# The opening constants of an mLSTM and mixture-of-experts kernel: moved between engines, built in another way, and all step ranks chosen anew

## The chip, the core and the metric

The kernel runs on one core of a Trainium2 chip. The metric is the device time of one execution in microseconds (us). The engines are named as the profile names them: PE is TensorE, DVE is VectorE (V in the code), ACT is ScalarE (A), POOL is GpSimd (G), and SP is SyncE, which here only issues DMAs.

## What is computed

Three layers in a row on 4 x 768 tokens: an mLSTM attention with 8 heads of 40, a leaky two-layer network with 2048 hidden units, and a top-1 mixture of 8 experts with 1024 hidden units. Cut to what matters here:

```python
for t in range(S):                      # _attn_ref, B=4, H=8, S=768, D=40
    m_new = np.maximum(f_gate[:, :, t] + m, i_gate[:, :, t])
    f_stab = np.exp(f_gate[:, :, t] + m - m_new)
    i_stab = np.exp(i_gate[:, :, t] - m_new)
    m = m_new
    C = f_stab * C + i_stab * outer(vt, kt)
    n = f_stab * n + i_stab * kt
    y[:, :, t] = sigmoid(o_gate[:, :, t]) * (C @ qt) / max(abs(n . qt), 1)

h = x @ w_in                            # _moe_ref, x: 3072 x 320, d_ff 2048
x2 = (max(h, 0) + alpha * min(h, 0)) @ w_out

xn, en = normalised x2, normalised expert_emb     # _moe2_ref, 8 experts
e = argmax(xn @ en.T / tau)
out = softmax weight of e * (max(x2 @ w1[e], 0) @ w2[e])
```

The recurrence over t is not run step by step: the gates of all 32 (batch, head) rows go through two scans, and the attention then works on chunks of 128 tokens, with a decay matrix that is the exponential of an argument made on PE.

## The kernel before

The 3072 tokens are 24 chunks of 128 (`NCH`), six for each of the four batches. Each chunk passes through the attention steps (`plan_chunk`: `load`, `loadt`, `mrow`, `arg0`, `arg1`, `exp0`, `exp1`, `s`, `p0`, `p1`, `phi`, `plo`, `u`, `c`, `o`, `tot`, `y`, `xhi`, `xlo`, `xt`). The transposed result goes to the first dense network (`m1` against `w_in_p`, `m2` against `w_out_p`, chunks taken in groups of one or two), then to the router, and after a sort by expert to the slots of the second network (`e1`, `e2`). Matrix factors are split into a high and a low half-precision part, so that DVE, ACT and POOL have work for every PE step. The weights of the first network arrive as 8-byte floats and are turned into 4-byte ones on DVE: `pconv` (its instructions stand in `to_f32`, on lines 632, 634 and 636) takes two pieces, that is six DVE instructions; there are 5 such pairs of `w_in` (512 columns a piece) and 8 pairs of `w_out` (320 columns a piece). The experts' weights are prepared later in 56 units (`ul`, `uh`, `uo`, `us`).

**The opening.** Before any planned step, the function issues instructions that write constants, in the order of the source. An engine takes its instructions in the order issued.

- POOL: `ident` and `iot` (lines 238 to 243), then `argL` filled with 0 and its first 27 rows with 1 (lines 371, 372), the two `argR` tiles, each a fill and three selections of 128 x 1024 (lines 374 to 377), `eye` and `low` (lines 378 to 384), one `qk` tile, `cf`, `vs`, `xs`, `x2s`, `ones`, `tri` and more, and last, because `g_set()` is called at line 1288 just before the plan is made, the gates' constants `keep` and `r0` (lines 277 to 279).
- DVE: four small instructions that need `iot`, then two `qk` tiles (line 388).
- SP and ACT begin with DMAs.

`argL` and `argR` are the two factors of the decay argument: `argL` gets three row groups from DRAM in `g_rows` and `argR` gets three rows in `mrow`, the rest of them is constant.

**The gates.** `g_load` brings `f_gate` and `i_gate`. `g_scan` on DVE (lines 291 to 295) multiplies by `keep` and adds `r0` in its scans. From it follow `g_top`, `g_res`, `g_mid`, `g_low` (three bf16 parts of two vectors), `g_store` to DRAM (line 311), `g_rows` back into `argL` (line 315), and beside it `g_w`, `g_wexp`, `g_wt`, `g_wt2`, `g_dec`, `g_dec2`. No `arg` step can run before `g_rows`, and the first `m1` needs the first chunk's `xt`.

**The order.** All steps after the opening are put in order by `Plan.order()` while the program is being written; at run time each engine simply takes its steps in that order and waits where data is late. The planner keeps a time for each engine, begins these clocks at `START`, and at each turn takes, among the steps that could start within `AHEAD` = 0.03 us of the first one, the one with the largest rank. A step's rank is its longest remaining path by the plan's own costs, plus `lean(k)`: `LEAN[name]`, plus `SOON[name]` if the step's index is below 4, plus `FIRST[name]` if it is below 2. `PACE` adds to the rank along the chain of the experts' units, `UNITS` gives the earliest planned time of each unit's load, and `EARLY` is a gap on a link from each `xt` to the first `m1` of its group:

```python
first_of = {k: rank[k] + lean(k) for k in steps}
...
plan.link(("xt", i), ("m1", chunk_group[i][0], 0), EARLY if i > 3 else 0.0)
```

Of the kernel before, what the change touches and what calls it, by code (L numbers as in the profile page):

```python
# [9 lines left out]
F32 = mybir.dt.float32  # L10
# [3 lines left out]
ALU = mybir.AluOpType  # L14
# [4 lines left out]
P = 128  # L19
B, H, S, D = 4, 8, 768, 40  # L20
# [20 lines left out]
class Plan:  # L41
# [7 lines left out]
    START = {"T": 0.5, "V": 2.0, "A": 2.0, "G": 4.9, "S": 1.2}  # L49
# [104 lines left out]
    "alpha": -35.4, "alpha2": -17.1, "arg0": 37.2, "arg1": 40, "c": -45.5, "cd": 75.6, "consts": 48.9, "e1":  # L154
    -115.6, "e2": -110.4, "ehi": 141.4, "elo": -9.4, "eout": -111.3, "ep": 81.6, "exp0": 58.9, "exp1": 15.6,
    "ey": 136.4, "g_dec": 51.6, "g_dec2": 33, "g_load": 150, "g_low": 2.9, "g_mid": -81.7, "g_res": -148.1,
    "g_rows": 115.9, "g_scan": 18.2, "g_store": -150, "g_top": 149.8, "g_w": 56.8, "g_wexp": -47.5, "g_wt":
    74.6, "g_wt2": 93.9, "gate": 147.1, "lane": -48.9, "lanes": -124.3, "load": 54.7, "loadt": 97.7, "logits":
# [3 lines left out]
    "psplit": -62.9, "rank": 38.5, "rexp": 71.5, "rload": -12.6, "rnorm": -63.7, "rsq": 150, "s": 84.9,  # L162
# [19 lines left out]
}  # L182
FIRST = {
    "alpha": -15.8, "alpha2": -80, "arg0": 54.7, "arg1": -22.7, "c": -80, "cd": 19.3, "consts": 69.7, "e1": 2,
    "e2": 80, "ehi": -29.6, "elo": 6.4, "eout": 68.2, "ep": -33.9, "exp0": 39.2, "exp1": 59.4, "ey": -9.1,
    "g_dec": -8.5, "g_dec2": 7.7, "g_load": -80, "g_low": -72.3, "g_mid": -56.1, "g_res": -4.9, "g_rows":
    -68.4, "g_scan": 7.4, "g_store": -23.2, "g_top": 80, "g_w": 80, "g_wexp": 24, "g_wt": -51.8, "g_wt2": -80,
    "gate": -77.9, "lane": 21.6, "lanes": 0.2, "load": 70.7, "loadt": -45.9, "logits": -57.1, "m1": 76.5,
    "m1f": 25.5, "m1h": 29.5, "m1l": 0.7, "m1r": -80, "m2": 80, "max": 69.2, "mrow": 80, "norm": -80, "norm2":
    22.6, "o": -35.1, "open": 25.2, "p0": -66.5, "p1": 80, "pconv": 49.1, "phi0": 69.8, "phi1": 43.2, "plo0":  # L190
    73, "plo1": -75.6, "pload": 80, "plow": 57.8, "pput": 45.1, "psplit": 13.3, "rank": 18, "rexp": -30.8,
    "rload": 75.9, "rnorm": -11.9, "rsq": 79.6, "s": -28.8, "scale": -59.9, "sort0": 22.8, "sort1": -80,
# [16 lines left out]
def kernel(  # L209
# [24 lines left out]
    ctx.enter_context(tc.manual_schedule())  # L234

# [4 lines left out]
                    pattern=[[-1, 32]], channel_multiplier=1)  # L240
# [23 lines left out]
    gt = {}  # L264

    def g_set():
# [83 lines left out]
    gp_ = ctx.enter_context(tc.tile_pool(name="gp", bufs=2))  # L350
# [7 lines left out]
    qk = [att.tile([P, 2, H // 2, P], F32, name=f"qk{i}") for i in range(NQ)]  # L358
# [20 lines left out]
    G.affine_select(out=eye, in_=eye, compare_op=ALU.not_equal, fill=1.0, base=0,
                    pattern=[[-1, P]], channel_multiplier=1)  # L380
# [460 lines left out]
    def x2_zero():  # L841
# [9 lines left out]
                    pattern=[[1, P]], channel_multiplier=-1)  # L851
# [132 lines left out]
    lane = const.tile([P, NCH], F32, name="lane")  # L984
# [303 lines left out]
    g_set()  # L1288
# [141 lines left out]
```

## Time and profile before

| | us |
|---|---|
| median of 3 runs | 736.11 |
| the runs | 735.71, 736.11, 743.06 |
| the profiled execution | 738.54 |
| its span, first to last instruction | 736.8 |
| PE busy | 639.4 (87%) |
| DVE busy | 464.5 (63%) |
| POOL busy | 362.2 (49%) |
| ACT busy | 335.4 (46%) |

The span lies inside the profiled execution's own time; 1.7 us lie around it. Times in the rows further down count from the start of the span. A busy share of the whole span says little here, since the kernel has stages: the opening and the gates, a stretch in which weights are converted and the first chunks go through, a long stretch of dense work on PE, and a tail of scattered writes.

### The profile page before, as it was taken

The page shows a single profiled execution, that of the slowest core. Times are in us where ns is not written, and L with a number is a line of the kernel's source. Part 1 is how long each engine was busy: PE and PEld are TensorE (multiplying, and loading weights), DVE is VectorE, ACT ScalarE, POOL GpSimd, SP SyncE. Part 2 cuts the span into 40 slices and gives each one's busy share as a digit, 9 for nine tenths or more (in the row PEclk, how much of TensorE's full clock was granted, in tenths as well). Part 3 has the DMA queues.
Part 4 walks back from the last instruction along what each step waited for, and adds up shares of the span by engine and source line. Part 5 has one row for each costly group of instructions (what it writes and reads, how often), then busy time and mean ns, then how long its engine had stood idle before and what let it go on. Part 6 is the DMA issues. An engine that isn't in the chain of part 4 may idle for free. (4 is left out here: it accounts for less than half of the span.)

```text
span 736.8 us, 17794 instructions
## 1 busy us (share of the span) xinstructions
PE 639.4 (87%) x6903; PEld 525.7 (71%) x6903; DVE 464.5 (63%) x1113; ACT 335.4 (46%) x666; POOL 362.2 (49%) x433
## 2 busy tenths in 40 slices
PE   0037567899999999989999999999999999999995
PEld 0024465677878778768878888887788887888884
DVE  1896988586889978966879887895346121121211
ACT  1335565455755675655575666533222222222221
POOL 9774769564655655635454645535311332323321
PEclk9999789899999999999999999999999999999999
DMA  8255534258669978788877875548755999999843
GB/s 269 91 166 125 168 115 137 81 165 216 222 198 215 247 228 210 211 188 240 225 228 195 254 196 168 140 149 267 213 183 161 266 252 302 360 326 315 214 120 64
DMA packets 109225, 149.02 MB, mean 202 GB/s; under 512 B 72215, under 2 KB 84416, under 8 KB 105298
## 3 DMA queue, kind: packets, MB, share of 16 engines
q1 hardware_dynamic: 81730, 83.22, 43.2%
q10 hardware_dynamic: 24128, 54.54, 23.6%
q0 software_dynamic: 3280, 10.10, 4.4%
q8 instruction: 56, 0.92, 0.5%
q14 instruction: 31, 0.25, 0.1%
HBM read 143.57 MB, written 30.46 MB: 236 GB/s over the span
## 5 line engine op out<-in xcount | busy, mean ns | idle before, releaser
L742 PE MATMUL hp<-xt,w_in_p 128*128 128x256 f16 (+1 forms) x1664 | 186.4, 267 | 19.9 <-DVE r L755 16.0
L742 PEld LDWEIGHTS <-w_in_p 128*128 128x128 f16 x1664 | 151.7, 99 | 43.2 <-DVE r L755 17.7
L762 POOL TENSOR_TENSOR g<-r,g 128x512 f16<-128x512 f32 (+1 forms) x104 | 118.2, 1141 | 118.8 <-ACT g L759 111.9
L830 PE MATMUL o<-w_out_p,g 128*128 128x320 f16 x1152 | 170.8, 302 | 2.7 <-DVE r L755 2.2
L830 PEld LDWEIGHTS <-g 128*128 128x128 f16 x1152 | 112.4, 99 | 48.6 <-DVE r L755 2.9
L755 DVE SCALAR_TENSOR_TENSOR r<-r,al,hp 128x256 f32<-128x256 f32 (+1 forms) x208 | 85.3, 453 | 30.5 <-ACT r L749 30.3
L1216 DVE SCALAR_TENSOR_TENSOR h<-hp,h 128x512 f16<-128x512 f32 x48 | 32.7, 689 | 112.6 <-ACT h L1212 103.3
L759 ACT ACTIVATE g<-r 128x512 f16<-128x512 f32 (+1 forms) x104 | 61.7, 594 | 70.3 <-DVE r L755 59.3
L749 ACT ACTIVATE r<-hp 128x512 f32<-128x512 f32 (+1 forms) x104 | 57.9, 557 | 46.0 <-PE hp L742 41.1
L1227 PEld LDWEIGHTS <-h 128*128 128x128 f16 x648 | 61.5, 98 | 23.3 <-ACT h L1212 1.1
L480 POOL TENSOR_TENSOR ph<-mb,ph 128x512 f16<-128x512 f32 x48 | 65.4, 1369 | 25.1 <-ACT ph L477 21.1
L1233 POOL DMA_INDIRECT out_dram<-y,idx x27 | 27.5, 1017 | 82.1 <-DMA out_dram<-y,idx 64.1
L1212 ACT ACTIVATE h<-hp 128x512 f16<-128x512 f32 x48 | 28.1, 596 | 81.6 <-PE hp L1207 76.8
L1182 POOL DMA_INDIRECT xg<-x_d,idx x31 | 30.5, 984 | 60.1 <-ACT y L1230 51.6
L1207 PEld LDWEIGHTS <-wr 128*128 128x128 f16 x896 | 51.5, 98 | 1.8 <-issue 0.5
L1207 PEld LDWEIGHTS <-w_in_p 128*128 128x128 f16 x832 | 48.0, 98 | 3.5 <-issue 2.2
L1207 PE MATMUL hp<-xt,w_in_p 128*128 128x128 f16 x768 | 46.1, 219 | 1.9 <-DMA xt<-xg 1.4
L1207 PE MATMUL hp<-xt,wr 128*128 128x128 f16 x768 | 46.1, 219 | 0.2 <-DMA xt<-xg 0.2
L1227 PE MATMUL o<-w_out_p,h 128*128 128x320 f16 x288 | 42.2, 299 | 0.2 <-issue 0.2
L1227 PE MATMUL o<-wr,h 128*128 128x320 f16 x288 | 42.1, 299 | 0.0
L552 POOL TENSOR_TENSOR y<-y,rd 128x320 f32<-128x320 f32 x24 | 19.6, 816 | 34.9 <-DVE y L547 29.3
L477 ACT ACTIVATE ph<-mb 128x512 f16<-128x512 f32 x48 | 29.6, 625 | 10.7 <-DVE mb L472 7.1
(206 smaller groups left out, 1036.3 us busy)
## 6 DMA issues: line engine op xcount, KB each, us to landing
wr<-wp SPq DMA_DIRECT2D x32, 1280.0 KB
w_in_p<-wp SPq DMA_DIRECT2D x15, 1280.0 KB
w_out_p<-wp SPq DMA_DIRECT2D x15, 1280.0 KB
kvo_t<-in_kvo_dram SPq DMA_DIRECT2D x24, 576.0 KB
ust<-in_moe_w_dram ACTq DMA_DIRECT2D x32, 320.0 KB
wp<-wo ACTq DMA_DIRECT2D x32, 320.0 KB
ust<-in_moe_w_dram ACTq DMA_DIRECT2D x16, 512.0 KB
wp<-wo ACTq DMA_DIRECT2D x16, 512.0 KB
```

Of the source, the lines that this page charges most:

```text
L477: A.activation(st["P", i][:, 0, j], st["mb", i][:, j], AF.Copy)
L480: G.tensor_tensor(st["P", i][:, 1, j], st["mb", i][:, j], st["P", i][:, 0, j], ALU.subtract)
L742: T.matmul(hp[:, a, :n], lhsT=w_in_p[:, wk, f], rhs=xt[:, xk], start=z == 0, stop=z == 7)
L749: A.activation(r, e_t[j, m], AF.Relu, scale=-1.0)
L755: V.scalar_tensor_tensor(r[:, a], r[:, a], al1[:, m + a:m + a + 1], hp[:, a], ALU.mult, ALU.add)
L759: A.activation(g_t[j][:, 0, m:m + 2], e_t[j, m], AF.Copy)
L762: G.tensor_tensor(g_t[j][:, 1, m:m + 2], e_t.pop((j, m)), g_t[j][:, 0, m:m + 2], ALU.subtract)
L830: T.matmul(o[:, :DM], lhsT=g[:, gi, k, tt], rhs=w_out_p[:, k, a], start=z == 0, stop=z == 47)
L1182: G.indirect_dma_start(out=xg, out_offset=None, in_=src, in_offset=bass.IndirectOffsetOnAxis(ap=idx[:, j:j + 1].bitcast(U32), axis=0))
L1207: T.matmul(hp[:, m], lhsT=w[:, wk, f], rhs=xt[:, xk], start=z == 0, stop=z == 7)
L1216: V.scalar_tensor_tensor(hs[:, 1], hp, 0.0, hs[:, 0], ALU.max, ALU.subtract)
L1227: T.matmul(o, lhsT=h[:, hi, k], rhs=w[:, k, a], start=z == 0, stop=z == 23)
```

## The change

- `START`, the planner's beginning times, go from V 2.0, A 2.0, G 4.9, S 1.2 to V 7.0, A 1.0, G 8.0, S 1.0.
- All of `LEAN`, `SOON` and `FIRST`, and `PACE` (5.15 to 6.16), `UNITS` ((121.6, 5.63) to (115.5, 5.75)) and `EARLY` (-1055.3 to -1184.1) have new values.
- `g_set()` is called right behind its definition, ahead of the other constants, and its three fills are on DVE. The pool `gp_` is opened earlier for it.
- `argL` is filled on DVE. `argR` is no longer filled and selected on POOL at full size: POOL fills a 128 x 8 tile `ind` and makes three selections on it, and DVE copies it, broadcast over 128 columns, into both `argR` tiles.
- The `qk` tiles 0 and 1 are filled on DVE, tile 2 on POOL, behind `ind` (before: 1 and 2 on DVE, 0 on POOL).

```diff
-    START = {"T": 0.5, "V": 2.0, "A": 2.0, "G": 4.9, "S": 1.2}
+    START = {"T": 0.5, "V": 7.0, "A": 1.0, "G": 8.0, "S": 1.0}
...
 LEAN = {
-    60, "m1": 18.6, "m1f": 149, "m1h": -51.5, "m1l": -14.3, "m1r": 105.8, "m2": 18.6, "max": -7.4, "mrow":
-    145.1, "norm": -66.9, "norm2": -112.7, "o": 54.3, "open": -150, "p0": 53.4, "p1": -44.8, "pconv": -48.3,
...
+    "max": 135.6, "mrow": 33.5, "norm": -34.1, "norm2": 127.7, "o": 11.5, "open": 21.6, "p0": -138.9, "p1":
+    25.6, "pconv": -49.4, "phi0": 118.8, "phi1": 112.6, "plo0": 74.1, "plo1": 122.4, "pload": -19.6, "plow":
...
 SOON = {
-    "norm": -16.7, "norm2": -70.9, "o": -80, "open": -65.6, "p0": 80, "p1": 70.8, "pconv": 73.3, "phi0": -80,
...
+    -62.3, "o": 23.2, "open": -3.2, "p0": 35, "p1": 61.3, "pconv": 22.9, "phi0": 28.8, "phi1": -14, "plo0":
...
 FIRST = {
-    22.6, "o": -35.1, "open": 25.2, "p0": -66.5, "p1": 80, "pconv": 49.1, "phi0": 69.8, "phi1": 43.2, "plo0":
...
+    "norm": 77.1, "norm2": -57.9, "o": 4.6, "open": -80, "p0": -80, "p1": 76.1, "pconv": 65.1, "phi0": 62.8,
...
-PACE = 5.15
-UNITS = (121.6, 5.63)
+PACE = 6.16
+UNITS = (115.5, 5.75)
...
-EARLY = -1055.3
+EARLY = -1184.1
...
+    gp_ = ctx.enter_context(tc.tile_pool(name="gp", bufs=2))
...
-        G.memset(gt["keep"], 1.0)
-        G.memset(gt["keep"].rearrange("p (c t) -> p c t", t=P)[:, :, 0:1], 0.0)
-        G.memset(gt["r0"], 0.0)
+        V.memset(gt["keep"], 1.0)
+        V.memset(gt["keep"].rearrange("p (c t) -> p c t", t=P)[:, :, 0:1], 0.0)
+        V.memset(gt["r0"], 0.0)
+
+    g_set()
...
-    gp_ = ctx.enter_context(tc.tile_pool(name="gp", bufs=2))
...
-    G.memset(argL, 0.0)
-    G.memset(argL[0:27], 1.0)
-    for x in argR:
-        G.memset(x, 0.0)
-        for k in range(3):
-            G.affine_select(out=x, in_=x, compare_op=ALU.not_equal, fill=1.0, base=-8 * k,
-                            pattern=[[-1, H], [0, P]], channel_multiplier=1)
+    for x in qk[:2]:
+        V.memset(x, 0.0)
     G.memset(eye, 0.0)
...
-    for x in qk[:1]:
+    ind = const.tile([P, H, 1], F32, name="ind")
+    G.memset(ind, 0.0)
+    for k in range(3):
+        G.affine_select(out=ind, in_=ind, compare_op=ALU.not_equal, fill=1.0, base=-8 * k,
+                        pattern=[[-1, H], [0, 1]], channel_multiplier=1)
+    V.memset(argL, 0.0)
+    V.memset(argL[0:27], 1.0)
+    for x in argR:
+        V.tensor_copy(x, ind.to_broadcast([P, H, P]))
+    for x in qk[2:]:
         G.memset(x, 0.0)
-    for x in qk[1:]:
-        V.memset(x, 0.0)
...
-    g_set()
     add(("g_load",), "S", 0.85, g_load, dma=0.6)
```

## Rows read from the trace of the kernel before

**Rows 1.** The page: the span, and PE in 40 slices, in tenths.

```profile
span 736.8 us, 17794 instructions
PE   0037567899999999989999999999999999999995
```

**Rows 2.** Busy time by stretch: start:end, length, PE, PEld, DVE, ACT, POOL, PEclk, DMA.

```profile
0.00:21.00 21.00, 0.00 (x0) 0.00 (x0) 2.35 (x7) 2.12 (x3) 19.55 (x43) 1.00 0.85 262
21.00:81.00 60.00, 22.94 (x154) 15.90 (x155) 51.05 (x81) 25.89 (x49) 37.66 (x34) 0.95 0.48 131
81.00:140.00 59.00, 42.54 (x496) 34.98 (x496) 48.19 (x116) 33.16 (x84) 44.07 (x100) 0.85 0.39 117
140.00:680.00 540.00, 525.37 (x5657) 434.04 (x5655) 353.30 (x898) 261.84 (x509) 244.84 (x244) 1.00 0.79 224
680.00:737.00 57.00, 48.57 (x604) 40.73 (x600) 9.59 (x14) 12.35 (x22) 16.11 (x17) 0.97 0.54 140
```

**Rows 3.** Timeline, POOL in the opening: start, us, instruction, idle before.

```profile
1.28 2.65 POOL L371 MEMSET argL<- 128x3072 bf16 x1
...
7.60 3.42 POOL L376 TENSOR_SCALAR_AFFINE_SELECT argR<-argR 128x1024 bf16<-128x1024 bf16 x3
...
15.34 0.20 POOL L378 MEMSET eye<- 128x128 bf16 x1
...
20.02 0.14 POOL L853 IOTA rev<- 128x8 f32 x1
...
20.15 0.73 POOL L277 MEMSET gates_a<- 32x768 f32 x1
20.94 0.10 POOL L278 MEMSET gates_a<- 32x6 f32 x1
20.98 0.73 POOL L279 MEMSET gates_a<- 32x768 f32 x1
```

**Rows 4.** Timeline, DVE in the same stretch.

```profile
2.11 0.91 DVE L388 MEMSET qk<- 128x1024 f32 x1 [0.16 <-issue]
3.19 0.91 DVE L388 MEMSET qk<- 128x1024 f32 x1 [0.16 <-issue]
4.04 0.06 DVE L291 MEMSET gates_a<- 32x1 f32 x1
21.07 1.75 DVE L292 TENSOR_TENSOR_SCAN gates_a<-gates_a 32x768 f32<-32x768 f32 x1 [16.97 <-POOL gates_a L278]
```

**Rows 5.** Timeline, single DVE instructions after the opening.

```profile
47.10 0.33 DVE L875 MEMSET ep<- 128x320 uint32 x1
...
48.12 0.21 DVE L882 CAST ep<-em 8x128 f16<-8x128 f32 x1
...
52.29 0.41 DVE L632 TENSOR_SCALAR w<-wst 128x512 int32<-128x512 int32 x1
...
64.81 0.50 DVE L536 COPY tot<-op 128x328 f32<-128x328 f32 x1 [1.17 <-PE op L518]
```

**Rows 6.** DMA queues from 0 to 12 us: packets, MB, share.

```profile
q10 hardware_dynamic: 476, 1.69, 48.2%
q1 hardware_dynamic: 322, 1.16, 36.2%
```

**Rows 7.** Timeline: storing the gates, the first argument, the first m1.

```profile
40.15 3.09 SPq L311 DMA_DIRECT2D pc_d<-gates_a  x1
...
56.11 0.58 PE L439 MATMUL ap<-argR,argL 128*128 128x512 bf16 x1 [6.99 <-DMA argL<-pc_d]
...
80.93 1.86 PE L742 MATMUL hp<-xt,w_in_p 128*128 128x128 f16 x16 [3.62 <-ACT mb L448]
```

**Rows 8.** DVE groups by line and shape, 20 to 145 us: busy, mean ns.

```profile
L634 DVE SCALAR_TENSOR_TENSOR w<-wst,w 128x320 int32<-128x320 int32 x16 | 9.8, 654 | 0.0
...
L632 DVE TENSOR_SCALAR w<-wst 128x320 int32<-128x320 int32 x16 | 8.5, 573 | 0.0
...
L636 DVE SCALAR_TENSOR_TENSOR w<-wst,w 128x320 int32<-128x320 int32 x16 | 8.2, 553 | 0.0
```

More of the change, by code (lines that the diff above doesn't have):

```diff
@@ L153 @@
 LEAN = {
[L154 to L158, printed above, removed]
[3 rows of a table removed]
@@ L162 @@
-    "psplit": -62.9, "rank": 38.5, "rexp": 71.5, "rload": -12.6, "rnorm": -63.7, "rsq": 150, "s": 84.9,
[4 rows of a table removed]
+    "alpha": 150, "alpha2": 111.9, "arg0": -42.1, "arg1": -22.1, "c": 12.3, "cd": -127.5, "consts": -37.5,
+    "e1": -117.8, "e2": -27.1, "ehi": 117.1, "elo": -12.1, "eout": -93.7, "ep": 93, "exp0": 51.5, "exp1":
+    -85.8, "ey": 64.4, "g_dec": -70.5, "g_dec2": 140.3, "g_load": -8.4, "g_low": -25.6, "g_mid": -22.1,
+    "g_res": 136, "g_rows": 3.5, "g_scan": -136, "g_store": -150, "g_top": -126.8, "g_w": -33.5, "g_wexp":
@@ L167 @@
+    -148.7, "g_wt": 127, "g_wt2": -143.3, "gate": 52.5, "lane": 112.3, "lanes": -71.9, "load": -23.1, "loadt":
[3 rows of a table added]
+    -126.5, "pput": -7.5, "psplit": 100.9, "rank": -29.4, "rexp": 10.4, "rload": -150, "rnorm": 116.3, "rsq":
[4 rows of a table added]
 }
 SOON = {
-    "alpha": 32.9, "alpha2": 51.1, "arg0": -17.9, "arg1": -62.5, "c": -49.1, "cd": 80, "consts": -15.3, "e1":
-    -12.9, "e2": -15, "ehi": -80, "elo": -8.8, "eout": 80, "ep": -11.7, "exp0": 49.6, "exp1": 5.4, "ey":
-    -64.5, "g_dec": -26.1, "g_dec2": -46, "g_load": -20.6, "g_low": -54.3, "g_mid": 80, "g_res": -61.2,
@@ L172 @@
-    "g_rows": -36.9, "g_scan": 70, "g_store": 34.8, "g_top": -80, "g_w": -43.9, "g_wexp": -58.7, "g_wt":
-    -20.6, "g_wt2": 71.4, "gate": -4.8, "lane": -78, "lanes": 41.1, "load": -46.3, "loadt": -77.6, "logits":
-    2, "m1": 32.5, "m1f": 70.1, "m1h": -57.9, "m1l": 29.9, "m1r": -76.6, "m2": 78.2, "max": 80, "mrow": 5,
-    "norm": -16.7, "norm2": -70.9, "o": -80, "open": -65.6, "p0": 80, "p1": 70.8, "pconv": 73.3, "phi0": -80,
-    "phi1": 80, "plo0": 39.1, "plo1": 9.6, "pload": 34.8, "plow": 58.7, "pput": -64, "psplit": -68.5, "rank":
@@ L177 @@
-    -7.9, "rexp": -79.6, "rload": 79.8, "rnorm": -34.3, "rsq": 29.7, "s": 48.9, "scale": -6.5, "sort0": 80,
[4 rows of a table removed]
+    "alpha": 0.3, "alpha2": 55.5, "arg0": 80, "arg1": -13.2, "c": -76.1, "cd": 80, "consts": 69.8, "e1": -75,
+    "e2": 80, "ehi": -1.9, "elo": 55.2, "eout": -31.5, "ep": -31.6, "exp0": -41.5, "exp1": -38.4, "ey": 54.9,
+    "g_dec": 2.9, "g_dec2": 80, "g_load": 43, "g_low": 74.5, "g_mid": -73.7, "g_res": -57.2, "g_rows": 80,
+    "g_scan": -28.5, "g_store": 49.2, "g_top": -51.9, "g_w": 74.8, "g_wexp": 50, "g_wt": 6.5, "g_wt2": 68.8,
@@ new lines @@
+    "gate": -20.4, "lane": 77.8, "lanes": -28.8, "load": -80, "loadt": -4.4, "logits": 14.2, "m1": 80, "m1f":
+    -80, "m1h": 62, "m1l": -61.5, "m1r": -20.8, "m2": 5.6, "max": 76.8, "mrow": -80, "norm": -24.3, "norm2":
+    -62.3, "o": 23.2, "open": -3.2, "p0": 35, "p1": 61.3, "pconv": 22.9, "phi0": 28.8, "phi1": -14, "plo0":
+    64.2, "plo1": 80, "pload": 53.6, "plow": 8.3, "pput": -80, "psplit": -53.3, "rank": -20.2, "rexp": 30.8,
+    "rload": 53.2, "rnorm": -61.7, "rsq": -38.9, "s": 68.1, "scale": 27, "sort0": -71.6, "sort1": -6.3,
[4 rows of a table added]
@@ L182 @@
 }
 FIRST = {
[L184 to L188, printed above, removed]
@@ L189 @@
-    "m1f": 25.5, "m1h": 29.5, "m1l": 0.7, "m1r": -80, "m2": 80, "max": 69.2, "mrow": 80, "norm": -80, "norm2":
-    22.6, "o": -35.1, "open": 25.2, "p0": -66.5, "p1": 80, "pconv": 49.1, "phi0": 69.8, "phi1": 43.2, "plo0":
-    73, "plo1": -75.6, "pload": 80, "plow": 57.8, "pput": 45.1, "psplit": 13.3, "rank": 18, "rexp": -30.8,
-    "rload": 75.9, "rnorm": -11.9, "rsq": 79.6, "s": -28.8, "scale": -59.9, "sort0": 22.8, "sort1": -80,
[3 rows of a table removed]
+    "alpha": -26.9, "alpha2": -28.1, "arg0": 50.2, "arg1": 37.2, "c": -80, "cd": -60.3, "consts": 80, "e1":
@@ new lines @@
+    -56.3, "e2": 69, "ehi": -52.9, "elo": 80, "eout": 36.9, "ep": 25.3, "exp0": -48.3, "exp1": 63.7, "ey":
+    68.1, "g_dec": -56.9, "g_dec2": -45.2, "g_load": -42, "g_low": -49, "g_mid": 49.2, "g_res": 43.1,
+    "g_rows": -11, "g_scan": -0.9, "g_store": 53.3, "g_top": 80, "g_w": 55.3, "g_wexp": -57, "g_wt": -62.6,
+    "g_wt2": -5.6, "gate": -72.4, "lane": 80, "lanes": 58.1, "load": -70.2, "loadt": -9.3, "logits": -80,
+    "m1": 80, "m1f": 80, "m1h": 46.5, "m1l": -13.9, "m1r": 19.8, "m2": -19.2, "max": 38.2, "mrow": -41.2,
@@ L196 @@
+    "norm": 77.1, "norm2": -57.9, "o": 4.6, "open": -80, "p0": -80, "p1": 76.1, "pconv": 65.1, "phi0": 62.8,
+    "phi1": 18, "plo0": -80, "plo1": 16.7, "pload": 47.7, "plow": -35.5, "pput": 23.5, "psplit": -53.2,
+    "rank": 18.6, "rexp": -34.3, "rload": 73.9, "rnorm": 80, "rsq": 0.4, "s": -80, "scale": 41.4, "sort0": 80,
[4 rows of a table added]
 }
 LOOK = 3.6
-PACE = 5.15
-UNITS = (121.6, 5.63)
+PACE = 6.16
+UNITS = (115.5, 5.75)
 SORTS = ((12, 4), 0)
 WARM = (12, 3)
-EARLY = -1055.3
+EARLY = -1184.1
 CHUNK = ("load", "loadt", "mrow", "arg0", "arg1", "exp0", "exp1", "vhi", "vlo",
```

25 rows, old and new, of tables (FIRST, LEAN, SOON) are left out of this document.

## The prediction

> **What bounds the kernel now.** I read the slices of the page first [rows 1]: PE has two empty slices, then four half-filled ones, and is at 9 tenths from the ninth slice on to the last. The busy time by stretch says it in numbers [rows 2]. From 140 to 680 us PE is busy 525.4 of 540 us at a granted clock of 1.00, which is its upper level, 2.4 GHz: there PE is the bound, and only 14.6 us are idle. From 680 on 8.4 us are idle. Before 140 us PE is idle 140 - 22.9 - 42.5 = 74.5 us. So three quarters of all PE idle time (97.5 us) lies in the front, and there another engine sets the pace.
>
> In the first 21 us that engine is POOL: busy 19.6 us, while DVE has 2.4 us of work and PE none [rows 2]. The timelines show why. POOL works through its constants from the top; the argL and argR tiles alone fill it from 1.28 to 15.34 us, and the gates' constants come last, from 20.15 to 21.7 us [rows 3]. DVE has filled its qk tiles by 4.1 us and then stands 16.97 us in front of the gate scan, released by POOL's line 278 [rows 4]. (The page's releaser is exact enough: the other operand, r0 on line 279, is first read by the later scan.) Nothing else on DVE can pass the scan, because an engine keeps its order, so the conversions of weights wait behind it too.
>
> From 21 to 140 us DVE is busy 51.1 + 48.2 = 99.2 of 119 us [rows 2], the busiest of the five there. The scan at 21.07 leads to the store of the gates at 40.15, to the first argument at 56.11 and the first m1 at 80.93 [rows 4, 7]. A stretch with one engine 83% busy and a chain of dependent steps in it can be shifted as a whole; that is the base of the forecast.
>
> **The change part by part.** *DVE's new opening.* Up to 2.11 us nothing changes (four small instructions that need iot). Then, in the order of the new source:
>
> - keep, 768 elements; its 6 columns; r0, 768. The two fills on DVE that the trace has are 1024 elements in 0.91 us and 320 in 0.33 us [rows 4, 5]: 0.83 ns an element and 0.06 us fixed. So 0.70 + 0.06 + 0.70, with the fixed part for the 6 columns: 1.5 us. POOL's 0.73 for the same shape [rows 3] agrees.
> - two qk tiles, as before: (4.04 - 2.11) / 2 = 0.97 us each [rows 4], 1.9 us.
> - argL with zeros. 3072 two-byte elements. The ep fill is 640 two-byte zeros in the code and stands in its row as 320 elements of uint32 [rows 5], so 1536 elements: 1.34 us. If it is not so rewritten, 2.62 us.
> - argL's 27 rows with 1.0: between 1.34 us, if this too is done in pairs, and 2.62 us for 3072 elements one by one. I take 2.62, because the only rewritten fill in a row is one of zeros; on POOL, argL, which is filled twice, takes 2.65 us [rows 3].
> - two argR copies, 1024 elements, f32 to bf16. The trace has no such copy. Lower bound: the CAST of 128 elements in 0.21 us and the one-source instruction of 512 in 0.41 us [rows 5] give 0.52 ns an element, so 0.68 us. Upper bound: the copy of 328 elements from PSUM in 0.50 us [rows 5], 1.5 ns an element, so 1.6 us. Source and target lie in SBUF as in the first two, so I take 0.68, both 1.4 us.
>
> Sum: 2.11 + 1.5 + 1.9 + 1.34 + 2.62 + 1.4 = 10.9 us, and with the one-column fill of line 291 the scan starts at 10.95 instead of 21.07. **The scan is 10.1 us earlier.** Cheapest values everywhere: 9.6 us on the clock, 11.5 earlier. Dearest (zeros 2.62, copies 1.6 each): 14.0 us, 7.1 earlier.
>
> The ones deserve a second look: by the Trainium skill, page VectorE: DVE Perf Modes, section Zero memsets can be issued as uint32 (trn2), a fill takes a cycle per element whatever the type, and only a fill of zero can be issued as uint32. The ep row agrees for zero, and no row here shows the case of ones. By the rule the scan starts at 10.95, and if it did not hold, at 9.7; the forecast would be 1.3 us lower.
>
> *POOL.* Taken off: everything from 1.28 to 15.34 us, 14.1 us, and the gates' 1.55 us [rows 3]. Added: ind, a fill and three selections of 128 x 8, at 0.14 us by the IOTA of that size [rows 3], about 0.6 us. POOL's remaining opening, from 15.34 to 20.15, takes 4.8 us. POOL is then through at 1.28 + 4.8 + 0.6 = 6.7 us. Its work hides behind DVE's 10.9 us; if it were not hidden it would only matter for ind, which DVE reads at 9.5 us and which is written ahead of the qk and cf fills, near 3 us. So the copies wait for nothing.
>
> *What is late next at the scan.* The gate loads: f_gate, issued at 0.81, had landed by 4.04, since the fill of line 291 overwrites its first column [rows 4]. In the new order SP may issue the loads of qk, which wait for DVE's fills up to 5.5 us, ahead of the gates; even then two issues and at most the 3.2 us to landing seen before end ahead of 10.9. Behind the scan, the first conversion needs two pieces of 512 KB: by 12 us each of the two hardware queues had moved more than that (1.69 and 1.16 MB) [rows 6]. Neither takes the scan's place as the bound.
>
> *What the argL and argR work costs on DVE.* 5.4 us of the 10.9 stand ahead of the scan for tiles whose rows arrive only before 56.11 [rows 7]. This is the part of the opening that is not gained.
>
> *The planner's numbers.* START issues nothing; it only moves the plan's clocks. EARLY changes nothing at all: each xt already precedes that m1 by a dependency, whose term in the rank is larger than one with a gap below -1000, before and after. LEAN, SOON, FIRST, PACE and UNITS add and remove no instruction; they reorder every queue (SP's and ACT's with their DMAs too). PE's work is the same, so a new order is worth what it does to the 97.5 us of PE idle time. The long stretch has at most 14.6 us to give. I put the new order at nothing, with both signs open, and keep the width for the range.
>
> *The sum.* The shift of 10.1 us passes through to the end, because the front is a DVE-bound chain and the stretch behind it is PE-bound without another clock of its own. The profiled execution, 738.54, would come to 728.4. It lies 2.4 us above the median of the runs; from the median: 736.11 - 10.1 = **726.0 us**.
>
> **The rivals.**
>
> *The order gives more.* The front still holds 64 us of PE idle time after the shift. An order that feeds PE there 8% better wins 5 us more: 721 us. For it: in the front DVE keeps 20 of 119 us free [rows 2]. Against: DVE's work there has to be done in any order.
>
> *The order gives the gain back.* Its place is DVE's queue between the gates and the first xt. The lean of p0 of chunk 0 is 53.4 + 80 - 66.5 = 66.9 before and -138.9 + 35 - 80 = -183.9 after; that of the w_out conversions stays near -49. So where both can start, conversions now go ahead of the first chunk's product, which no m1 can do without. The eight pairs take 9.8 + 8.5 + 8.2 = 26.5 us, 3.3 a pair [rows 8]. Three pairs more ahead of p0 make 9.9 us: 736 us, no change. For it: the size of that swing, 251 us. Against: a conversion done early needn't be done later, and DVE is 82% busy from 81 to 140 us [rows 2], so most of it comes back.
>
> *Slower.* The same mechanism, with the time not given back. The first m1 then comes later than now. Two pairs stay below 1%; slower by 7.4 us takes 10.1 + 7.4 = 17.5 us, so from 5.3 pairs on. With six pairs: 736.1 - 10.1 + 19.9 = 745.9 us.
>
> *The scan doesn't move.* That needs a wait on something other than POOL up to 21 us; the loads above leave no room for it. I give it nothing of its own.
>
> **How the numbers follow.** About 1% (7.4 us) is what a measurement of this kernel can tell from no change; that is 728.7 and 743.5 us. The shift with a neutral order, 721 to 731 us: 0.47, of which 0.09 lie above 728.7 (the dear end of DVE's opening alone gives 729). The better order, below 721: 0.19. The gain given back, 731 to 743.5: 0.22. Slower: 0.12. So faster 0.38 + 0.19 = 0.57, the same 0.09 + 0.22 = 0.31, slower 0.12. The likeliest case has 721 to 731 as its own range. The range for 8 in 10 runs from 715 to 742 us: it leaves out the far end of the better order and nearly all of the slower case.
>
> **What would show it.** In the profile after: the scan of line 292's counterpart at 10 to 14 us, with DVE busy and not waiting ahead of it; the ones fill at 2.6 us, and the argR copies at 0.7 (over 1.1 would be the upper row's kind); POOL's opening ended near 7 us; the store of the gates near 30, the first argument near 46 and the first m1 near 71 us; PE idle before 140 us at about 64. Wrong would be: a scan near 11 us and a first m1 that is not earlier (then the new queue order took it, to be seen in what DVE does between them), or a front that is 10 us shorter and a stretch behind it with well over 14.6 us of PE idle time.

## The result and the profile after

The changed kernel took 727.97 us (median of 6 runs, 727.02 to 729.69), against 736.76 us for the kernel before on the same chip (median of 6, 731.94 to 743.06). The ratio is 0.9883, with a 95% interval from 0.9834 to 0.9932, that is 5.0 to 12.2 us. Ratios are estimated without the few runs that fell in a slower state, so they differ a little from the quotient of two medians (0.9881 here). So it is faster, by 8.8 us between the medians; 726.0 had been forecast, and the range 715 to 742 holds it.

The page after: the span, and PE in 40 slices (compare [rows 1]).

```profile
span 728.0 us, 17810 instructions
PE   0137568999999989999999999999989999999995
```

Busy time by stretch after (start:end, length, then PE, PEld, DVE, ACT, POOL, each with its number of instructions, PEclk, DMA share, GB/s), for [rows 2]:

```profile
0.00:21.00 21.00, 2.77 (x16) 2.27 (x16) 16.00 (x24) 2.97 (x3) 8.23 (x36) 1.00 0.79 210
21.00:81.00 60.00, 26.62 (x196) 19.76 (x197) 50.33 (x89) 28.86 (x57) 39.18 (x38) 0.86 0.63 178
81.00:140.00 59.00, 45.04 (x517) 38.54 (x517) 48.40 (x111) 35.28 (x87) 39.23 (x100) 0.82 0.51 131
140.00:680.00 540.00, 529.31 (x5689) 436.35 (x5687) 356.36 (x888) 259.09 (x503) 248.36 (x239) 0.99 0.79 220
680.00:728.00 48.00, 39.26 (x494) 33.35 (x491) 7.60 (x11) 10.23 (x18) 12.53 (x13) 0.95 0.58 155
```

Before 140 us PE is now idle 140 - 2.77 - 26.62 - 45.04 = 65.6 us instead of 74.5: 8.9 less. In the long stretch it is idle 10.7 us instead of 14.6, and behind it 8.7 instead of some 8.2. Against these 12.4 us of idle time that are gone stand 3.6 us more of busy time (643.0 against 639.4): the granted clock of the two stretches from 21 to 140 us is 0.86 and 0.82, where it was 0.95 and 0.85 [rows 2], so the same work takes longer there. That makes the 8.8 us between the two spans. It is one execution of each; two later profiled executions of the same kernel, on other chips, had spans of 736.5 and 735.3 us, so the split is good to some us only, and what follows goes by medians.

DVE's opening after: start, us, instruction, idle before and its releaser (compare [rows 4]).

```profile
2.05 0.70 DVE L279 MEMSET gates_a<- 32x768 f32 x1
...
4.91 0.91 DVE L375 MEMSET qk<- 128x1024 f32 x1 [0.16 <-issue]
6.09 1.34 DVE L388 MEMSET argL<- 128x1536 uint32 x1 [0.27 <-issue]
8.12 2.62 DVE L389 MEMSET argL<- 27x3072 bf16 x1 [0.69 <-DVE argL L388]
10.67 1.21 DVE L391 CAST argR<-ind 128x1024 bf16<-128x1024 f32 x2
13.59 0.17 DVE L1291 TENSOR_SCALAR al<-al 128x16 f32<-128x16 f32 x1 [1.71 <-DMA al<-in_moe_alpha_dram]
13.98 0.06 DVE L295 MEMSET gates_a<- 32x1 f32 x1 [0.21 <-DMA gates_a<-in_f_gate_dram]
14.07 1.75 DVE L296 TENSOR_TENSOR_SCAN gates_a<-gates_a 32x768 f32<-32x768 f32 x1
```

DVE works from 2 us on without a long pause, and POOL's opening constants end at 7.1 us (6.7 had been forecast). But the scan starts at 14.07, 7.0 us earlier than before [rows 4], not 10.1. Two waits stand ahead of it that the kernel before didn't have: for alpha, the leak of the first network, and for `f_gate`. SP's queue after shows why:

```profile
0.81 0.47 SPq L1288 DMA_DIRECT2D al<-in_moe_alpha_dram  x1
1.34 3.53 SPq L286 DMA_DIRECT2D gates_a<-in_f_gate_dram  x1
...
38.11 0.45 SPq L315 DMA_DIRECT2D pc_d<-gates_a  x1
```

The new ranks put the load of alpha first on SP, and its DVE instruction ahead of the scan. The load is issued at 0.81 and its reader goes at 13.59; the next issue on the queue, `f_gate`'s, takes 3.53 us, and its data too is there only near 13.98. (That alpha is the cause is shown further down, by moving it.) Before, alpha was loaded at 36.78 us.

From the scan to the first m1, after (DVE, POOL, PE, SP and ACT; [rows 7] has the counterparts of before):

```profile
19.01 3.84 POOL L325 TENSOR_TENSOR gates_b<-gates_b 32x640 f32<-32x640 f32 x1
...
21.65 4.33 DVE L305 SCALAR_TENSOR_TENSOR gates_a<-gates_b,gates_a 32x768 f32<-32x768 f32 x1
25.91 1.90 DVE L305 SCALAR_TENSOR_TENSOR gates_b<-gates_b,gates_a 32x768 f32<-32x768 f32 x1
...
47.56 0.63 PE L444 MATMUL ap<-argR,argL 128*128 128x512 bf16 x1
...
49.28 0.69 DVE L477 SCALAR_TENSOR_TENSOR mb<-sp,mb 128x512 f32<-128x512 f32 x1 [4.95 <-ACT mb L453]
...
66.84 1.22 SPq L571 DMA_TRANSPOSE xt<-xs  x1
...
81.00 0.47 ACT L647 ACTIVATE w<-w 128x320 f32<-128x320 f32 x1 [3.94 <-DVE w L641]
...
82.46 0.57 ACT L453 ACTIVATE mb<-ap 128x512 f32<-128x512 f32 x1
...
83.08 1.87 PE L747 MATMUL hp<-xt,w_in_p 128*128 128x128 f16 x16 [3.49 <-ACT mb L453]
```

The store comes at 38.11 (2.0 us earlier than before), the first argument at 47.56 (8.6 earlier), the first transposed chunk at 66.84 (8.4 earlier, it was 75.23), and the first m1 at 83.08, 2.2 us *later* than before. So the first m1 does not simply follow its own chunk. In the new order PE makes the attention of three chunks ahead of it, where it made two; by 81 us it has been busy 29.4 us with 212 matmuls instead of 22.9 us with 154 [rows 2]. And the row of m1 says what PE waits for at the end: `mb` on ACT (L453), which reads `ap`; the code gives `ap` and the product of m1 the same five buffers. On ACT that `mb` stands behind a pair of `w_out` conversions, for which ACT itself waits 3.94 us. Before, the first m1 waited for `mb` in the same way [rows 7], behind a pair of `w_out` too:

```profile
78.85 0.47 ACT L642 ACTIVATE w<-w 128x320 f32<-128x320 f32 x1 [3.48 <-DVE w L636]
```

But that was the first such pair, and now it is the third.

Two questions follow. Does the end follow the scan, as the forecast says, although m1 does not? And what do the new ranks do, which the forecast put at nothing?

### The profile page after: what moved, and what is told of

Its sections match the earlier page's. It is cut to its first block, busy times and chain, and to the rows that moved or that the text cites. A ratio compares the mean times of both kernels' runs of the same rounds, so it can differ in the third digit from the quotient of the medians.

```text
span 728.0 us, 17810 instructions
## 1 busy us (share of the span) xinstructions
PE 643.0 (88%) x6903; PEld 530.3 (73%) x6903; DVE 478.7 (66%) x1120; ACT 336.4 (46%) x666; POOL 347.5 (48%) x424
## 5 line engine op out<-in xcount | busy, mean ns | idle before, releaser
L747 PE MATMUL hp<-xt,w_in_p 128*128 128x256 f16 (+1 forms) x1664 | 190.0, 271 | 16.3 <-DVE r L760 7.3
L747 PEld LDWEIGHTS <-w_in_p 128*128 128x128 f16 x1664 | 153.7, 101 | 40.2 <-DVE r L760 14.5
L767 POOL TENSOR_TENSOR g<-r,g 128x512 f16<-128x512 f32 (+1 forms) x104 | 122.6, 1185 | 112.2 <-ACT g L764 109.2
L485 POOL TENSOR_TENSOR ph<-mb,ph 128x512 f16<-128x512 f32 x48 | 62.9, 1318 | 36.7 <-ACT ph L482 33.4
L1212 PEld LDWEIGHTS <-w_in_p 128*128 128x128 f16 x832 | 48.3, 98 | 1.4
L462 PE MATMUL sp<-qk 64*128 64x128 f32 x384 | 30.9, 301 | 18.9 <-DMA qk<-in_qk_t_dram 16.5
L462 PEld LDWEIGHTS sp<-qk 64*128 64x128 f32 x384 | 25.9, 201 | 26.0 <-DVE gates_a L296 16.5
```

The source lines that it names most:

```text
L462: T.matmul(sp[:, r, z], lhsT=x[w, 1, z], rhs=x[w, 0, z], start=True, stop=True)
L485: G.tensor_tensor(st["P", i][:, 1, j], st["mb", i][:, j], st["P", i][:, 0, j], ALU.subtract)
L747: T.matmul(hp[:, a, :n], lhsT=w_in_p[:, wk, f], rhs=xt[:, xk], start=z == 0, stop=z == 7)
L767: G.tensor_tensor(g_t[j][:, 1, m:m + 2], e_t.pop((j, m)), g_t[j][:, 0, m:m + 2], ALU.subtract)
L1212: T.matmul(hp[:, m], lhsT=w[:, wk, f], rhs=xt[:, xk], start=z == 0, stop=z == 7)
```

## The experiments

Every kernel was timed beside the kernel before on its own chip, and the ratios are to that. Times in the middle columns are starts from the profiled execution, in us.

| kernel | first scan | store issued | first argument | first m1 | median | ratio (95%) |
|---|---|---|---|---|---|---|
| before | 21.07 | 40.15 | 56.11 | 80.93 | 736.76 | 1 |
| after | 14.07 | 38.11 | 47.56 | 83.08 | 727.97 | 0.9883 (0.9834 to 0.9932) |
| open_only | 11.94 | 31.13 | 46.95 | 71.77 | 724.66 | 0.9851 (0.9798 to 0.9904) |
| ranks_only | 21.07 | 45.17 | 54.62 | 90.32 | 737.15 | 1.0028 (0.9990 to 1.0067) |
| alpha_late | 11.95 | 35.98 | 45.44 | 81.26 | 726.28 | 0.9895 (0.9839 to 0.9951) |
| delay_scan | 25.82 | 50.10 | 59.30 | 94.83 | 742.22 | 1.0092 (1.0053 to 1.0130) |
| light_opening | 5.88 | 33.49 | 45.55 | 70.38 | 731.07 | 0.9900 (0.9849 to 0.9950) |
| alpha_far | 11.94 | 31.02 | 47.49 | 72.31 | 730.32 | 0.9880 (0.9822 to 0.9937) |
| light_and_far | 5.88 | 27.79 | 44.81 | 69.62 | 727.86 | 0.9836 (0.9787 to 0.9884) |
| after_again | 14.15 | 39.99 | 49.45 | 85.27 | 733.56 | 0.9912 (0.9873 to 0.9950) |
| open_only_2 | 11.94 | 31.03 | 47.76 | 72.58 | 725.52 | 0.9856 (0.9804 to 0.9909) |
| after_3 | 13.80 | 37.88 | 47.29 | 82.59 | 729.43 | 0.9899 (0.9849 to 0.9949) |
| gates_only | 5.88 | 34.86 | 49.91 | 74.74 | 726.09 | 0.9843 (0.9791 to 0.9894) |
| act_copies | 5.88 | 26.22 | 42.10 | 66.92 | 718.10 | 0.9752 (0.9703 to 0.9800) |

The kernel before took 736.76 us (median) beside after, 734.57 beside open_only to delay_scan, 740.30 beside light_opening to after_again, and 736.92 beside the last four. Medians from different groups of these are therefore not compared. One kernel's times in the middle columns differ too from one execution to the next: the first m1 of the changed kernel by up to 2.7 us (three profiles), that of open_only by 0.8 (two).

### The change cut in two: the opening alone, the ranks alone

open_only is the changed kernel with the planner's old numbers, ranks_only the kernel before with the new ones:

```diff
-    START = {"T": 0.5, "V": 7.0, "A": 1.0, "G": 8.0, "S": 1.0}
+    START = {"T": 0.5, "V": 2.0, "A": 2.0, "G": 4.9, "S": 1.2}
...
-PACE = 6.16
-UNITS = (115.5, 5.75)
+PACE = 5.15
+UNITS = (121.6, 5.63)
```

> The new opening with all planner numbers of before, so the planned steps stand in the order of before. The alpha load is then late in SP's queue, and the scan should start when DVE's opening ends, near 11.9 us instead of 21.07. Theory shift (the whole program follows the scan): 736.8 - 9.1 = 727.6 us. Rival order (the gain of the change is the new order's, the front swallows an earlier scan): within 1% of the kernel before, 733 to 740 us.

> The old opening with all planner numbers of after, so the planned steps stand in the order of after. POOL's constants release the scan at about 21.1 us. Theory shift: the change moved the scan from 21.07 to 14.07, 7.0 us, of the 8.8 us that it gained, so the order alone is worth 1.8 us: about 735 us. Rival order: 728 us, as after.

open_only, timelines of DVE, POOL, SP and PE:

```profile
11.94 1.75 DVE L295 TENSOR_TENSOR_SCAN gates_a<-gates_a 32x768 f32<-32x768 f32 x1
...
16.89 6.38 POOL L324 TENSOR_TENSOR gates_b<-gates_b 32x640 f32<-32x640 f32 x1
...
20.33 0.94 DVE L304 SCALAR_TENSOR_TENSOR gates_a<-gates_b,gates_a 32x768 f32<-32x768 f32 x1
...
31.13 2.75 SPq L314 DMA_DIRECT2D pc_d<-gates_a  x1
...
46.95 0.58 PE L443 MATMUL ap<-argR,argL 128*128 128x512 bf16 x1 [6.94 <-DMA argL<-pc_d]
...
71.77 1.86 PE L746 MATMUL hp<-xt,w_in_p 128*128 128x128 f16 x16 [3.62 <-ACT mb L452]
```

Against [rows 4, 7] the scan is 9.13 us earlier, the first argument 9.16 and the first m1 9.16 (9.13, 8.35 and 8.35 in open_only_2): the front moves as one block. The end came 734.57 - 724.66 = 9.9 us earlier, and 11.4 in the repetition (open_only_2). That is the forecast's mechanism, alone.

ranks_only, timelines of DVE and PE:

```profile
13.50 0.76 DVE L1287 TENSOR_SCALAR al<-al 128x16 f32<-128x16 f32 x1 [9.40 <-DMA al<-in_moe_alpha_dram]
...
21.07 1.75 DVE L293 TENSOR_TENSOR_SCAN gates_a<-gates_a 32x768 f32<-32x768 f32 x1 [6.81 <-POOL gates_a L279]
...
28.66 4.33 DVE L302 SCALAR_TENSOR_TENSOR gates_a<-gates_b,gates_a 32x768 f32<-32x768 f32 x1
...
90.32 1.87 PE L743 MATMUL hp<-xt,w_in_p 128*128 128x128 f16 x16 [3.49 <-ACT mb L449]
```

With the old opening the wait for alpha hides, since POOL keeps the scan until 21.07 anyway. The new ranks by themselves give 1.0028: nothing, or a loss of up to 0.7%. Their first m1 is 9.4 us later than that of before and the end is the same to 2 us, so a time of the first m1 tells something of the end only between kernels of one order.

The same lines show what the new order does between scan and store: 24.1 us in ranks_only and 24.0 in the changed kernel, 19.1 in the kernel before and 19.2 in open_only. The instruction that makes the rest of the first vector (`g_res`, L302 and L305) takes 4.33 us in the new order and 0.94 in the kernel before and in open_only (2.00 in open_only_2), and the expert embedding's preparation, 4.2 us, stands ahead of the last `g_low`. Behind the store it is the other way: 9.45 us to the first argument in both kernels with the new order, 16.0 and 15.8 in those with the old, where the store's own issue takes 2.75 to 3.09 us and four stores of `w_in_p` stand on SP between it and the rows that it feeds.

### The wait for alpha, and the scan delayed on purpose

alpha_late is the changed kernel with alpha's load and its DVE instruction later in the finished order; delay_scan is the changed kernel with one fill of DVE's opening done nine times:

```diff
+    ks = plan.order()
+    for x, y in ((("alpha",), ("x2zero",)), (("alpha2",), ("scale",))):
+        ks.remove(x)
+        ks.insert(ks.index(y), x)
-    for k in plan.order():
+    for k in ks:
```

```diff
-    V.memset(argL, 0.0)
+    for _ in range(9):
+        V.memset(argL, 0.0)
```

> After, with the alpha load moved on SP's queue from ahead of the gate loads to just ahead of the zero row of x2, and its one DVE instruction from ahead of the scan to ahead of the router's scaling; all else in the same order. The gates should have landed before DVE's opening ends, and the scan start at 11.9 to 12.0 instead of 14.07. Theory shift: 728.0 - 2.1 = 725.9 us. Rival order: 728. If the gate loads are late for another reason than alpha, the scan stays near 14.

> After, with the zero fill of argL on DVE done nine times instead of once, so that the scan starts some 10.7 to 13 us later less the 2.1 us that it waits for loads now: 23 to 26 us. Same order of steps. Theory shift: the end moves by as much, 737 to 740 us. Rival order: the front has slack for it and the end stays within 3 us of 728.

alpha_late, DVE and PE:

```profile
11.95 1.75 DVE L296 TENSOR_TENSOR_SCAN gates_a<-gates_a 32x768 f32<-32x768 f32 x1
...
81.26 1.86 PE L747 MATMUL hp<-xt,w_in_p 128*128 128x128 f16 x16 [3.71 <-ACT mb L453]
```

delay_scan, DVE and PE:

```profile
25.82 1.75 DVE L296 TENSOR_TENSOR_SCAN gates_a<-gates_a 32x768 f32<-32x768 f32 x1
...
94.83 1.86 PE L748 MATMUL hp<-xt,w_in_p 128*128 128x128 f16 x16 [3.49 <-ACT mb L454]
```

The wait for alpha and `f_gate` is worth 14.07 - 11.95 = 2.1 us at the scan, and 2.1 at the store and at the first argument. At the end it can't be told from nothing (0.9895 and 0.9883, intervals of half a per cent to each side). Over a longer way it can: from alpha_late to delay_scan, on one chip, the scan is 13.9 us later, the first m1 13.6, and the end 742.22 - 726.28 = 15.9 us. Within one order the end follows the scan about one to one.

### How much of the opening is needed

light_opening is open_only with the fills and copies of `argL` and `argR` taken back from DVE; POOL does them, with each pair of two-byte ones written as one 4-byte number. alpha_far is open_only with alpha's load behind `g_rows` and its DVE instruction ahead of the first step that reads it. light_and_far does both.

```diff
-    V.memset(argL, 0.0)
-    V.memset(argL[0:27], 1.0)
-    for x in argR:
-        V.tensor_copy(x, ind.to_broadcast([P, H, P]))
...
+    G.memset(argL.bitcast(F32), 0.0)
+    G.memset(argL[0:27].bitcast(F32), 1.0019378662109375)
+    for x in argR:
+        G.tensor_copy(x, ind.to_broadcast([P, H, P]))
```

```diff
+    ks = plan.order()
+    ks.remove(("alpha",))
+    ks.insert(ks.index(("g_rows",)) + 1, ("alpha",))
+    ks.remove(("alpha2",))
+    ks.insert(ks.index(("m1f", 0, 0)), ("alpha2",))
```

> The kernel open_only (new opening, all planner numbers of before), with the fills of argL and the copies into argR taken off DVE and put on POOL, behind its cf fills; argL is filled as 4-byte elements there, two bf16 ones as one f32 of the same bits. DVE's opening then ends near 5.9 us instead of 11.9, POOL's near 12. Theory shift (everything follows the scan): 6.0 us earlier than open_only, near 718.7 us. Rival data: the first conversion, now due at 10.5 us, waits for its weight pieces, of which 1.05 MB of the 2.85 MB moved by 12 us are needed, or g_w waits for POOL's opening; then 1 to 3 us of it are lost and the time is 720 to 722 us. Rival order: open_only's 724.7.

> The kernel open_only with the alpha load moved on SP's queue from ahead of the zero row and the gates' store to behind the gates' rows, and its DVE instruction to ahead of the first one that uses it. In open_only the two issues behind alpha took 2.9 and 2.75 us, in after, without alpha ahead, 0.25 and 0.45 us. So the store is issued in 0.5 us at 31.1, and the rows land up to 4 us sooner, the first argument at 43 to 47 us. If the front follows the argument: 721 to 724 us. If DVE's conversions set it: first m1 at 71.8 as in open_only, and 724.7 us.

> Both edits on open_only: DVE's opening without argL and argR, and alpha behind the gates' rows. Theory shift: scan at 5.9 us, and the rows up to 4 us sooner relative to it: 715 to 719 us. If one of the two is covered by the other, 719 to 722.

alpha_far, SP:

```profile
31.02 0.33 SPq L314 DMA_DIRECT2D pc_d<-gates_a  x1
31.45 3.91 SPq L667 DMA_DIRECT2D w_in_p<-ttl  x1
...
40.24 0.58 SPq L420 DMA_DIRECT2D argR<-pc_d  x2
```

alpha_far shortened the store's issue from 2.75 to 0.33 us and gained nothing: the rows that wait for the store are issued at 40.24, where open_only had 39.76. The issue right behind the store now takes 3.91 us, 0.55 in open_only; why was not looked into. In light_opening the scan starts at 5.88, 6.1 us earlier than in open_only, and yet the store comes at 33.49: there alpha's load stands in front of it on SP, and the issue behind that load takes 6.22 us; its first argument and first m1 are 1.4 us ahead of open_only's. Together (light_and_far) the two bring the store to 27.79, the first argument 2.1 us and the first m1 2.2 us ahead of open_only. The median of light_and_far is 3.2 us below light_opening's on the same chip, with intervals of 3.6 us to each side: not told apart. Where more than half of the other 4 us of the earlier scan went shows in light_and_far, on DVE and POOL:

```profile
7.66 3.00 DVE L296 TENSOR_TENSOR gates_b<-gates_a 32x768 f32<-32x768 f32 x1
7.83 2.01 POOL L394 CAST argR<-ind 128x1024 bf16<-128x1024 f32 x2
```

Behind the first scan DVE's subtraction takes 3.00 us, where open_only's took 0.95, and the copy of five columns behind it 0.72 instead of 0.15. The second scan starts at 11.34; with the 2.85 us that open_only has between its two scans it would be 8.73.

### The gates' constants alone, and the copies on a third engine

gates_only is the kernel before with one part of the change: `keep` and `r0` first, and on DVE. act_copies is light_and_far with the two `argR` copies on ACT:

```diff
-        G.memset(gt["keep"], 1.0)
-        G.memset(gt["keep"].rearrange("p (c t) -> p c t", t=P)[:, :, 0:1], 0.0)
-        G.memset(gt["r0"], 0.0)
+        V.memset(gt["keep"], 1.0)
+        V.memset(gt["keep"].rearrange("p (c t) -> p c t", t=P)[:, :, 0:1], 0.0)
+        V.memset(gt["r0"], 0.0)
+
+    g_set()
```

```diff
-    for x in argR:
-        G.tensor_copy(x, ind.to_broadcast([P, H, P]))
...
+        if k == ("th", 0):
+            for x in argR:
+                A.activation(x, ind.to_broadcast([P, H, P]), AF.Copy)
```

> The kernel before with one part of the change alone: the gates' constants are filled first and on DVE; argL and argR stay on POOL, the planner's numbers are those of before. The scan should start near 5.9 us, 15.2 earlier. POOL is then busy to about 20.1 us, so g_w starts there, 5.6 us earlier than 25.74 of before, and DVE's two-input instructions may be held up by POOL's selections up to 15.3. Theory shift by the scan: 736 less 10 to 15, the best of all, 721 to 726 us. Rival POOL chain (g_w and what hangs on it sets the front): only 5 to 6 us faster, 730 to 731 us, so that moving argL and argR off POOL is needed for the rest.

> The kernel light_and_far with the two copies into argR on ACT, ahead of the first th, instead of on POOL. In light_and_far DVE's subtraction behind the first scan took 3.0 us instead of 0.95 while POOL made its copies (7.8 to 9.8 us). If these copies hold DVE up, the subtraction is back at 0.95 and the second scan starts at 8.5 to 8.9 instead of 11.34 us; the end moves by up to 2.5 us to 0.980 of the kernel before. If it waited for the i gate's load, it stays at 3 us and the time at 0.9836.

gates_only, POOL, DVE and PE:

```profile
7.60 5.55 POOL L378 TENSOR_SCALAR_AFFINE_SELECT argR<-argR 128x1024 bf16<-128x1024 bf16 x3
7.66 1.85 DVE L296 TENSOR_TENSOR gates_b<-gates_a 32x768 f32<-32x768 f32 x1
...
74.74 1.87 PE L744 MATMUL hp<-xt,w_in_p 128*128 128x128 f16 x16 [3.63 <-ACT mb L450]
```

gates_only gives 0.9843, as much as the whole opening on the same chip (0.9856). Its scan is 6.1 us earlier than open_only's, but POOL goes on with the large selections, and DVE and POOL slow each other: POOL's three selections take 5.55 us instead of 3.42 [rows 3], DVE's subtraction 1.85 instead of 0.95. The first m1 then comes 2.2 us later than in open_only_2.

act_copies, POOL, DVE, ACT and PE:

```profile
6.52 1.37 POOL L392 MEMSET argL<- 27x1536 f32 x1
7.66 0.95 DVE L296 TENSOR_TENSOR gates_b<-gates_a 32x768 f32<-32x768 f32 x1
8.05 2.00 ACT L1374 ACTIVATE argR<-ind 128x1024 bf16<-128x1024 f32 x2
...
66.92 1.87 PE L744 MATMUL hp<-xt,w_in_p 128*128 128x128 f16 x16 [3.63 <-ACT mb L450]
```

With the copies on ACT the subtraction is back at 0.95 us, though POOL's fills run beside it; the second scan starts at 9.24, and the first m1 at 66.92, 5.7 us ahead of open_only_2 and 2.7 ahead of light_and_far. The subtraction did not wait for the load of the i gate, then. A ratio of 0.980 had been expected. The end is 725.52 - 718.10 = 7.4 us earlier than that kernel's and 11.3 earlier than the changed one's on the same chip. This version beats both kernels: 0.9752 of before.

### The repetitions

> After itself, beside the three kernels above on one chip. 727 to 729 us, 1.1 to 1.3% faster than the kernel before; open_only's order is 2 to 4 us better if the new planner numbers cost time.

> The kernel open_only again, beside after on one chip. If the new planner numbers cost time on top of the new opening, as 0.9851 against 0.9883 and 0.9912 of the kernel before on three chips suggests: 2 to 5 us faster than after. If that difference is the chips': within 1 us of after.

> After again, beside open_only: 1.0 to 1.3% faster than the kernel before on this chip.

What they measured stands in the table. On one chip the changed kernel took 729.43 us (7 runs, 727.20 to 737.07) and open_only 725.52 (6 runs, 723.22 to 728.74), and their intervals against before overlap. But run against run open_only is the faster one in 36 of the 42 pairs, and the 3.9 us between the medians are in the 2 to 5 us that were expected if the new ranks cost time. So with the new opening they probably cost some us. Of the delay at the scan 2.1 us are the wait for alpha, though alpha_late, without it, was not measurably faster. The record shows another candidate, which was not tried by itself: the mean granted clock of the runs was 0.967 in after_3 and 0.976 in open_only_2, and 0.971 in ranks_only against 0.975 in the kernel before beside it.

## Why the prediction was right, and where it was not

**The mechanism held, for a scan that starts at 11.9 us or later.** There the front is a block that moves with the scan, and the stretch behind it has no clock of its own. The opening alone showed it (9.13, 9.16, 9.16 us, and 9.9 to 11.4 at the end), and so did the delayed scan (13.9 and 15.9). Below that other waits take over: light_opening's scan is 6.1 us earlier than open_only's and its first m1 only 1.4. The size came out short: 10.1 us were forecast, 8.8 were measured, and 6.7 and 7.5 in the two repetitions (medians). That is about the 7.0 us by which the scan moved; that the first measurement came within 2 us of 726.0 is in part luck.

**DVE's opening was priced right, and its gaps were missed.** All instructions came out as worked out: keep 0.70, qk 0.91, zeros 1.34, ones 2.62; the two copies took 1.21 together, where 1.4 was said, so each lies below the lower bound of 0.68. The trace agrees with the Trainium skill, page VectorE: DVE Perf Modes, section Zero memsets can be issued as uint32 (trn2), which speaks of zeros alone: the zeros ran as 1536 elements of uint32, the ones as 3072 of bf16. (The last section shows ones that the program itself writes in pairs.) The opening ended at 11.88 us instead of 10.9: the sum had no gaps between the instructions, among them 0.69 us in which the ones wait for the zeros under them. That is 1.0 us of the term of 10.1, whose size without the ranks was 9.13. One reading was loose: between the empty slices and the ninth stand six slices of 3 to 8 tenths [rows 1], not four half-filled ones; no number hangs on it.

**The step that failed is "What is late next at the scan".** It went through f_gate and the conversions' pieces and ended with "Neither takes the scan's place as the bound"; and of the rival that the scan doesn't move it said that "the loads above leave no room for it". It allowed for the loads of qk to go ahead of the gates', but for no other load, although all ranks were new, and it did not ask whether another instruction comes ahead of the scan on DVE. The alpha step did both, and cost 2.1 us (14.07 against 11.95 in alpha_late). It could have been read in the source, as p0's lean was: alpha's entry in `LEAN` goes from -35.4 to 150.

**The order at nothing: right in sum with the old opening, wrong in its parts.** There the new ranks alone gave 1.0028, from 0.999 to 1.0067; with the new opening they probably cost some us (above). Inside this zero are large terms of both signs: 4.9 us more from the scan to the store, 6.4 us less from the store to the first argument, and more attention on PE ahead of the first m1. The store at 30 and the first m1 at 71 us, which the forecast named as signs, came at 38.11 and 83.08; in open_only they are 31.13 and 71.77. Its own test for a wrong forecast, a scan near 11 and an m1 that is not earlier, would have misled: in alpha_late the scan is at 11.95, the m1 at 81.26 is not earlier than before, and the end is earlier all the same. The idle time of PE before 140 us, said to be about 64 us, was the better sign: 65.6.

**The rivals.** *The order gives the gain back* named conversions ahead of the first chunk's product. At that place it didn't happen: the product starts at 49.28, when its exponential is there, after 4.95 us of waiting with no conversion in the way. But two more pairs of `w_out` are done ahead of the first m1 than before (three against one), and that m1 is 2.2 us later. The end came earlier all the same; the reason that the rival gives against itself fits, that a conversion done early needn't be done later, but no run separates it. The slower case did not come. *The order gives more* is not borne out by ranks_only.

**"The part of the opening that is not gained."** It was put at 5.4 us; the scan of gates_only and light_opening shows 11.94 - 5.88 = 6.1 us. But taking the work off DVE again brought nothing measurable by itself (light_opening 0.9900, gates_only 0.9843, open_only 0.9851 and 0.9856), since POOL's or SP's part then came in between. It was gained in act_copies, where POOL only fills `argL`, ACT makes the copies and alpha's load is out of the way; the copies on ACT without moving alpha were not tried.

**What stays open.** The ends of gates_only and act_copies are 10.8 and 18.8 us earlier than before, their first m1 only 6.2 and 14.0 us. The intervals (7.8 to 15.4 and 14.7 to 21.9 us) begin just above these, so most of the difference can be noise. The profiles say where act_copies has it, in one execution of each kernel: 13.2 us less PE idle time before 140 us, 5.8 less in the long stretch, and 2.4 us less busy time. Why the long stretch gains was not looked for. Of the new ranks, only alpha was tried by itself; delaying the embedding's preparation or the instruction beside POOL's (below) in the new order was not.

## What to carry to other kernels

When a constant gates the first chain of a kernel, make it first and on the engine that reads it; here this part alone gave as much as the whole opening, and the larger tiles that came along to the same engine added nothing that could be measured and put off the scan by 6.1 us. When an order is chosen anew, go through the queue of each engine from the start up to the step that is to move, loads included: here a small transfer of scattered elements ahead of the scan cost 2.1 of the 9.1 us that the opening had won there. And judge such a change by where the end goes; a milestone in the middle tells something only between kernels that have the same order.

## What the runs showed of the hardware

**A load of single elements holds its queue.** Alpha's load takes 128 x 16 numbers of 4 bytes that are scattered in DRAM. From 0 to 6 us SP's queue after shows

```profile
q1 hardware_dynamic: 1342, 0.01, 12.4%
```

that is 1342 packets for 0.01 MB. The load's reader, which waited for it, started 12.8 us after its issue, and the next issue, `f_gate`'s, took 3.53 us; it takes 0.42 in alpha_late, where it stands ahead of alpha, and the scan no longer waits there. In all 14 profiles the issue right behind alpha's takes 2.06 (gates_only) to 6.22 us (light_opening). It is not the only long issue: alpha_far has one of 3.91 us with alpha behind it.

**DVE and POOL slow each other when both read SBUF.** SBUF holds all tiles of this kernel but the products of PE. `g_res` on DVE has two inputs there; in every kernel with the new order it starts beside POOL's subtraction (L325, 3.84 us) and takes 4.33 us, while POOL's next two instructions take 1.24 and 1.14 us. In open_only and the kernel before the same two meet, and it is POOL that is held up: the subtraction takes 6.38 us and `g_res` 0.94. Alone POOL's takes 1.25 us (gates_only, where DVE stands still beside it). So either of the two can be the one that waits. In light_and_far it was a copy on POOL that stretched DVE's subtraction to 3.00 us; in act_copies a fill on POOL, which only writes, left the subtraction at 0.95. By the Trainium skill, page SBUF — State Buffer, section Who interferes with whom, a VectorE instruction with two inputs in SBUF contends with a GpSimd instruction that reads SBUF, and not with one that only writes it. These runs agree, with the numbers above. A copy of five columns on DVE, with one input, did take longer beside such a fill: 0.67 us in act_copies against 0.15 in open_only, where POOL stood still.

**Ones can be filled in pairs.** POOL's fill of 27 x 3072 bf16 ones, written as 27 x 1536 4-byte numbers whose two halves are both a one, took 1.37 us (act_copies, L392), against 2.65 us for the 3072-element fill of that engine [rows 3] and 2.62 on DVE.
